# A gated mix of linear attention and a token-shifting MLP: the first x chunk turned by a DMA transpose, the opening loads reordered, later transposing loads cut smaller

## Chip, cores and metric

The kernel runs on one core of a Trainium2 chip. The metric is the device time of one execution in microseconds; the time before is the median of six runs.

## What is computed

The input x has 2048 rows of 640 columns (bfloat16). Branch A is linear attention with 32 heads of 20, branch B a token-shifting MLP; a sigmoid gate per row mixes them.

```python
x = A_x
g = sigmoid((x * gate_w).sum(-1, keepdims=True))

# branch A
q, k, v = heads of (x @ wqkv)                 # 640 -> 3 * 640
phi = lambda t: where(t > 0, t + 1, exp(t)) + 1e-6
pq, pk = phi(q), phi(k)
kv = einsum("bhsd,bhse->bhde", pk, v)
z = pk.sum(over rows)
a = (pq @ kv / (pq . z + 1e-6)) @ wo

# branch B
h = gelu(layernorm(x) @ w1)                   # then its four column groups are shifted
x1 = x + shifted(h) @ w2                      # by +1, -1, +2, -2 rows
b = x1 + gelu(layernorm(x1) @ w3) @ w4        # 640 -> 1728 -> 640

out = g * a + (1 - g) * b
```

## The kernel before

The 2048 rows are 16 chunks of 128 (`NCH`), the 640 columns five slices of 128 (`DC`). x is held twice: `x_sb` (tile RXH) with rows on the partitions, `xT` (tile RXT) turned, with columns on the partitions. The K weights lie in `wkg` (tile RA), 640 columns in five slabs by rows of wqkv. Two columns are added to them: column 640 is `gate_w`, so that the K product gives the gate's sum as well, and column 641 is one, which gives the row sums. `KW` is thus 642, and `k_mm(c, p, dc)` does one slice of chunk c in two matmuls, of 512 and of 130 columns, into the PSUM tile `PP[p]`. Each PSUM tile holds two banks of 512 columns.

All instructions of an engine run in the order in which the code issues them (`manual_schedule`); waits between engines are on semaphores. The stages follow one another on TensorE: K of all chunks (L334 to L350), with the first steps of G = x^T pk (`g_unit`, L261) mixed in from chunk 5 on; Q (L387) with the rest of G; w1 (L420), w2 (L553), and then w3 (L568), attention's product (L594) and w4 (L635) in two halves.

The opening works so:

- ACT's queue issues wk slabs 0, 1, 2 and 4, SP's queue x chunks 0, 1, 2 and wk slab 3 (L166 to L171). GpSimd's queue issues the load of `gate_w` into `g5` (L160).
- TensorE runs six warm-up matmuls on zeros (L305), then the transpose of a mask (L306), which ACT copies to `E4` (L307). It lies in `PP[0]`, the tile of chunk 0's K product.
- `x_tr(c, a, b)` turns chunk c on TensorE, five transposes into PSUM (L313), and copies the result to `xT`, three slices by VectorE (L314) and two by ACT (L315). Chunks 0, 1 and 2 go this way.
- After `x_tr(0, 3, 2)` a one-element memset on VectorE (L320) writes into chunk 3's place in `xT`. The transposing load of chunk 3 writes the same place, so SP waits there until the memset is done.
- `late_loads` then issues on SP, in one fixed order, the other chunks of x, transposing loads into `xT` (L157, from the input in device memory) taking turns with plain copies into `x_sb` (L154), and behind them wq (L290), w1, wv, wo and w2. `xT` of a chunk is read by that chunk's K product, `x_sb` by G and by the layernorm statistics.
- After `x_tr(1, 1, 2)` the gate's five values per partition are made by a transpose of `g5` (L324) and copied by VectorE into column 640 of the five slabs (L326). Then come K of chunk 0, slices 0 and 1, `x_tr(2, 3, 2)`, and the rest of K of chunks 0 to 2.

Of the kernel before, what the change touches and what calls it, by code (L numbers as in the profile page):

```python
# [16 lines left out]
def kernel(  # L17
# [27 lines left out]
    KW = D + 2  # L45
# [24 lines left out]
    x_sb = RXH[:, 0:NCH * D].rearrange("p (c d) -> p c d", c=NCH)  # L70
# [66 lines left out]
    def alloc():  # L137
        return free.pop(0)
# [11 lines left out]
    sp, aq = nc.sync, nc.scalar  # L150
    xv = x2.rearrange("(c p) d -> p c d", p=P)

    def load_x(c0, c1):
        sp.dma_start(x_sb[:, c0:c1, :], xv[:, c0:c1, :])  # L154

    def load_xT(c0, c1):
        sp.dma_start_transpose(xT[:, :, c0 * P:c1 * P], x2[c0 * P:c1 * P, :])  # L157
# [5 lines left out]
    def load_wk(q, dc):  # L163
        q.dma_start(wkg[:, dc, 0:D], A_wqkv[dc * P:(dc + 1) * P, D:2 * D])

    for dc in (0, 1, 2, 4):  # L166
        load_wk(aq, dc)
    load_x(0, 1)
    load_x(1, 2)
    load_x(2, 3)  # L170
    load_wk(sp, 3)  # L171


    nc.gpsimd.memset(mask4[:], 1.0)
# [72 lines left out]
        nc.vector.tensor_scalar(e[:, 0:n], e[:, 0:n], 1.0, 1e-6, op0=ALU.min, op1=ALU.add)  # L247
        nc.vector.scalar_tensor_tensor(dst, src, 0.0, e[:, 0:n], op0=ALU.max, op1=ALU.add)

    def k_mm(c, p, dc):  # L250
        for (n0, n1) in ((0, 512), (512, KW)):
            mm(PP[p][:, n0:n1], lhsT=xT[:, dc, c * P:(c + 1) * P], rhs=wkg[:, dc, n0:n1],  # L252
               start=(dc == 0), stop=(dc == DC - 1))

# [22 lines left out]
    def late_loads():  # L277
        load_xT(3, 4)
        load_xT(4, 5)
        load_x(3, 4)  # L280
        load_xT(5, 7)
        load_x(4, 6)
        load_xT(7, 9)
        load_x(6, 9)
        load_xT(9, 12)
        load_x(9, 12)
        load_xT(12, 16)
        load_x(12, 16)
        rows = lambda w, a, b: w[:, a:b].rearrange("(j p) d -> p j d", p=P)
        sp.dma_start(wq, rows(A_wqkv, 0, D))  # L290
        sp.dma_start(w1, rows(B_w1, 0, D))
        sp.dma_start(wv, rows(A_wqkv, 2 * D, 3 * D))
        sp.dma_start(wo6[0:GW, 0:5, :], A_wo[0:5 * GW, :].rearrange("(g r) d -> r g d", r=GW))
        sp.dma_start(wo6[0:gsz[5], 5, :], A_wo[5 * GW:D, :])
        sp.dma_start(w2[:, 0:4, :], B_w2.rearrange("(g c) d -> c g d", c=CG)[0:P])
        for g in range(4):
            sp.dma_start(w2[32 * g:32 * (g + 1), 4, :], B_w2[CG * g + P:CG * (g + 1), :])
        w1g = w1.rearrange("p k (g c) -> p k g c", c=CG)
        w1x4 = w1x.rearrange("p k (g c) -> p k g c", g=4)
        for g in range(4):  # L300
            nc.gpsimd.tensor_copy(w1x4[:, :, g, :], w1g[:, :, g, P:CG])


    for _ in range(6):
        mm(PP[3][:, 512:1024], lhsT=warm[:, 0:P], rhs=warm[:], start=True, stop=True)  # L305
    nc.tensor.transpose(PP[0][:, 0:64].bitcast(BF16), mask4[:], ident[:])  # L306
    act(E4[:], PP[0][:, 0:64].bitcast(BF16), ACT.Copy)  # L307
# [1 line left out]
    def x_tr(c, a, b):  # L309
        ta, tb = PP[a][:, 0:512].bitcast(BF16), PP[b][:, 0:512].bitcast(BF16)  # L310
        for dc in range(DC):
            t, k = (ta, dc) if dc < 3 else (tb, dc - 3)
            nc.tensor.transpose(t[:, k * P:(k + 1) * P], x_sb[:, c, dc * P:(dc + 1) * P], ident[:])  # L313
        nc.vector.tensor_copy(xT[:, 0:3, c * P:(c + 1) * P], ta[:, 0:3 * P].rearrange("p (j s) -> p j s", j=3))  # L314
        act(xT[:, 3:5, c * P:(c + 1) * P], tb[:, 0:2 * P].rearrange("p (j s) -> p j s", j=2), ACT.Copy)  # L315

    for _ in range(3):
        alloc()
    x_tr(0, 3, 2)
    nc.vector.memset(xT[:, 0, 3 * P:3 * P + 1], 0.0)  # L320
    late_loads()
    x_tr(1, 1, 2)
    tg = PP[3][:, 512:1024].bitcast(BF16)
    nc.tensor.transpose(tg[:, 0:DC], g5[0:DC, :], ident[0:DC, 0:DC])  # L324
    for dc in range(DC):
        nc.vector.tensor_copy(wkg[:, dc, D:D + 1], tg[:, dc:dc + 1])  # L326
    k_mm(0, 0, 0)
    k_mm(0, 0, 1)
    x_tr(2, 3, 2)
    k_mm(1, 1, 0)  # L330
    k_mm(1, 1, 1)
    k_mm(2, 2, 0)
    k_mm(2, 2, 1)
    for c in range(3):  # L334
# [7 lines left out]
    for c in range(3, NCH):  # L342
        p = alloc()
# [37 lines left out]
    for half in range(2):  # L381
        for j in range(DC):
            p = alloc()
# [301 lines left out]
```

## Time and profile before

| | us |
|---|---|
| time, median of 6 runs | 267.65 |
| lowest and highest of the 6 | 267.49, 268.2 |
| the profiled execution's own time | 268.05 |
| its span, from first to last instruction | 266.3 |
| TensorE busy (share of the span) | 261.0 (98%) |
| VectorE, ACT, GpSimd busy | 116.0, 110.7, 32.8 |
| granted TensorE clock, mean | 1.0 |

The span is what the profile's views cover; the time is that of the whole execution as the device reports it. Times in the views are counted from the first instruction. TensorE's busy time counts matmuls from start to modelled end, so overlapping ones are counted once. A line such as L252 is the line of the code that issued the instruction; where a helper is called from many places, they share its line. An instruction of a DMA queue (SPq, ACTq) is shown for the time that it held the issuing queue, and its landing is given apart, counted from the start of the issue.

### The profile page before, as it was taken

How to read it: one execution, taken by the hardware profiler on the slowest of the kernel's cores; microseconds unless marked ns; L12 is line 12 of the kernel's file. 1: busy time of each engine (PE TensorE's matmuls, PEld its weight loads, DVE VectorE, ACT ScalarE, POOL GpSimd, SP SyncE). 2: the span in 40 equal slices, each digit the busy share in tenths (PEclk: the TensorE clock that was granted, in tenths of full speed). 3: DMA queues.
4: the chain of work that ended last, by engine and by line, in shares of the span. 5: the costliest groups of instructions: out<-in, count | busy, mean ns of one | idle time of the engine just before them, and what ended most of it. 6: DMA issues, size and time to landing. Idle time of an engine off the chain costs nothing.

```text
span 266.3 us, 4224 instructions
## 1 busy us (share of the span) xinstructions
PE 261.0 (98%) x1699; PEld 135.4 (51%) x1699; DVE 116.0 (44%) x212; ACT 110.7 (42%) x165; POOL 32.8 (12%) x111
## 2 busy tenths in 40 slices
PE   6999999999999999999999999999999999999995
PEld 2555555555545445554444455555544444555552
DVE  2486748665655065999920033233200002233232
ACT  3466663665355771244977522022034444022020
POOL 5000222020200000536870000000000000000000
PEclk9999999999999999999999999999999999999999
DMA  6999993431340269942652001001000000001001
GB/s 203 182 233 252 362 225 67 62 75 25 77 98 0 60 214 363 312 81 49 101 100 49 0 2 49 27 25 49 27 25 0 2 0 0 25 27 49 27 25 49
DMA packets 42149, 23.95 MB, mean 90 GB/s; under 512 B 30994, under 2 KB 41362, under 8 KB 42130
## 3 DMA queue, kind: packets, MB, share of 16 engines
q1 hardware_dynamic: 41378, 22.99, 35.2%
q10 hardware_dynamic: 720, 0.69, 0.8%
q8 instruction: 13, 0.21, 0.4%
q14 instruction: 6, 0.05, 0.1%
q0 software_dynamic: 32, 0.00, 0.0%
HBM read 12.86 MB, written 3.44 MB: 61 GB/s over the span
## 4 chain that ended last, share of the span: by engine, by line
PE 96%; DMA 2%; DVE 0%; issue 0%; POOLq 0%
PE pp L635 20%; PE pp L568 19%; PE pp L252 8%; PE pp L420 8%; PE pp L594 8%; PE pp L387 8%; PE pp L553 8%; PE pp L261 8%; DMA g<-in_gate_w_dram 2%; PE pp L577 2%; PE pp L620 1%; PE pp L629 1%; PE pp L584 1%; PE pp L454 1%; PE pp L440 1%; PE pp L361 0%
## 5 line engine op out<-in xcount | busy, mean ns | idle before, releaser
L635 PE MATMUL pp<-RB,RXH 128*128 128x512 bf16 (+1 forms) x390 | 54.4, 299 | 0.0
L568 PE MATMUL pp<-lnxT,RA 128*128 128x512 bf16 x240 | 52.1, 379 | 0.0
L635 PEld LDWEIGHTS <-RXH 128*128 128x128 bf16 x390 | 29.6, 98 | 24.2 <-issue 2.1
L568 PEld LDWEIGHTS <-RA 128*128 128x128 bf16 x240 | 23.4, 98 | 28.0
L597 ACT ACTIVATE RXH<-pp,g_all 128x640 f32<-128x640 f32 x16 | 12.7, 793 | 54.9 <-PE pp L594 54.9
L570 ACT ACTIVATE RXH<-pp 128x1024 bf16<-128x1024 f32 x24 | 24.2, 1019 | 26.7 <-PE pp L568 26.7
L244 ACT ACTIVATE eb<-pp 128x640 bf16<-128x640 f32 (+1 forms) x26 | 21.4, 828 | 25.3 <-PE pp L387 16.3
L261 PE MATMUL pp<-RPK,RXH 128*128 128x512 bf16 (+1 forms) x160 | 25.2, 299 | 0.0
L252 PE MATMUL pp<-RA,RXT 128*128 128x512 bf16 (+1 forms) x160 | 24.0, 300 | 0.0
L387 PE MATMUL pp<-RXT,RA 128*128 128x512 bf16 x100 | 23.3, 379 | 0.0
L594 PE MATMUL pp<-Mp,pqT 128*128 128x512 bf16 (+1 forms) x160 | 23.1, 299 | 0.0
L599 DVE SCALAR_TENSOR_TENSOR RPK<-RPK,omg,RXH 128x640 f32<-128x640 f32 x8 | 7.1, 885 | 36.5 <-ACT RXH L597 36.5
L553 PE MATMUL pp<-w,RXH 128*128 128x512 bf16 (+1 forms) x160 | 21.9, 299 | 0.0
L420 PE MATMUL pp<-lnxT,RB 128*128 128x512 bf16 x80 | 18.3, 379 | 0.0
L261 PEld LDWEIGHTS <-RXH 128*128 128x128 bf16 x160 | 12.7, 98 | 10.4
L247 DVE TENSOR_SCALAR eb<-eb 128x640 bf16<-128x640 bf16 (+1 forms) x26 | 9.5, 364 | 19.4 <-ACT eb L244 19.4
L599 DVE SCALAR_TENSOR_TENSOR RXT<-RXT,omg,RXH 128x640 f32<-128x640 f32 x8 | 7.1, 885 | 24.6 <-ACT RXH L597 24.6
L594 PEld LDWEIGHTS <-pqT 128*128 128x128 bf16 x160 | 12.2, 98 | 10.0 <-issue 0.8
L252 PEld LDWEIGHTS <-RXT 128*128 128x128 bf16 x160 | 12.3, 98 | 9.6 <-DVE RA L326 0.2
L553 PEld LDWEIGHTS <-RXH 128*128 128x128 bf16 x160 | 12.3, 98 | 9.5
L604 DVE SCALAR_TENSOR_TENSOR RXH<-pp,omg,RXT 128x640 bf16<-128x640 f32 x8 | 7.1, 884 | 19.8 <-PE pp L635 19.8
L387 PEld LDWEIGHTS <-RA 128*128 128x128 bf16 x100 | 11.1, 118 | 8.9
(110 smaller groups left out, 237.4 us busy)
## 6 DMA issues: line engine op xcount, KB each, us to landing
out_dram<-RXH SPq DMA_DIRECT2D x15, 160.0 KB, 1.8
RA<-in_B_w_dram SPq DMA_DIRECT2D x5, 432.0 KB, 7.0
RA<-in_A_wqkv_dram SPq DMA_DIRECT2D x2, 800.0 KB, 8.6
RB<-in_B_w_dram SPq DMA_DIRECT2D x1, 1120.0 KB
RXH<-in_A_x_dram SPq DMA_DIRECT2D x2, 480.0 KB, 4.9
RB<-in_B_w_dram SPq DMA_DIRECT2D x1, 960.0 KB, 12.8
RB<-in_B_w_dram SPq DMA_DIRECT2D x1, 800.0 KB, 8.2
Mp<-Mscr SPq DMA_DIRECT2D x1, 800.0 KB
```

Source lines behind the costliest of these rows:

```text
L244: act(e[:, 0:n], src, ACT.Exp)
L252: mm(PP[p][:, n0:n1], lhsT=xT[:, dc, c * P:(c + 1) * P], rhs=wkg[:, dc, n0:n1], start=(dc == 0), stop=(dc == DC - 1))
L261: mm(PP[p][:, n0:n1], lhsT=x_sb[:, c, i * P:(i + 1) * P], rhs=pk[:, c, n0:n1], start=(c == 0), stop=(c == NCH - 1))
L387: mm(PP[p][:, tt * 512:(tt + 1) * 512], lhsT=wqp[:, dc, j], rhs=xT[:, dc, t0:t0 + 512], start=(dc == 0), stop=(dc == DC - 1))
L420: mm(PP[p][:, tt * 512:(tt + 1) * 512], lhsT=lh, rhs=lnxT[:, dc, t0:t0 + 512], start=(dc == 0), stop=(dc == DC - 1))
L553: mm(PP[p][:, n0:n1], lhsT=hsT[:, fc, 2 + c * P:2 + (c + 1) * P], rhs=w2[:, fc, n0:n1], start=(fc == 0), stop=(fc == DC - 1))
L568: mm(PP[p][:, k * 512:(k + 1) * 512], lhsT=w3[:, dc, (fc + k) * P:(fc + k + 1) * P], rhs=lnxT[:, dc, t * 512:(t + 1) * 512], start=(dc == ...
L570: act(h2T[:, t % 2, fc:fc + 2, :], PP[p][:].rearrange("p (k s) -> p k s", k=2), ACT.Gelu_apprx_tanh)
L594: mm(PP[p][:, n0:n1], lhsT=pqT[:, j, c * P:(c + 1) * P], rhs=Mp[:, j, n0:n1], start=(j == 0), stop=(j == DC - 1))
L597: act(ga, PP[p][:, 0:D], ACT.Copy, scale=g_all[:, c:c + 1])
L599: nc.vector.scalar_tensor_tensor(x1(c), x1(c), omg[:, c:c + 1], ga, op0=ALU.mult, op1=ALU.add)
L635: mm(PP[p][:, n0:n1], lhsT=h2T[:, k, fc, cc], rhs=w4[:, fc, n0:n1], start=False, stop=(fc == NF - 1))
```

## The change

Chunk 0 is no longer loaded as rows and turned on TensorE: a transposing load of chunk 0 into `xT` is the first instruction on SP's queue. x chunks 1 and 2 move to ACT's queue, between wk slabs 0 and 1 and after slab 1; slabs 2, 3 and 4 are on SP's, behind the transpose. A seventh warm-up matmul is added. `k_mm` gets an argument that chooses the 512-wide or the 130-wide part: for chunks 0 and 1, slices 0 and 1, the wide parts are issued first, two of them ahead of the gate's transpose, and the four narrow parts, which read the gate column, afterwards. `x_tr(0, ...)` is gone, the marker memset stands after `x_tr(1, 1, 2)`. In `late_loads` a plain copy of chunk 0 into `x_sb` is added, and the transposing loads are of 1, 1, 1, 1, 1, 2, 1, 2 and 3 chunks, where they were of 1, 1, 2, 2, 3 and 4. What is computed is the same.

```diff
-    for dc in (0, 1, 2, 4):
-        load_wk(aq, dc)
-    load_x(0, 1)
-    load_x(1, 2)
-    load_x(2, 3)
-    load_wk(sp, 3)
+    load_xT(0, 1)
+    load_wk(aq, 0)
+    aq.dma_start(x_sb[:, 1, :], xv[:, 1, :])
+    load_wk(aq, 1)
+    aq.dma_start(x_sb[:, 2, :], xv[:, 2, :])
+    for dc in (2, 3, 4):
+        load_wk(sp, dc)
...
-    def k_mm(c, p, dc):
-        for (n0, n1) in ((0, 512), (512, KW)):
+    def k_mm(c, p, dc, part=(0, 1)):
+        for (n0, n1) in (((0, 512), (512, KW))[k] for k in part):
...
         load_xT(3, 4)
         load_xT(4, 5)
+        load_x(0, 1)
         load_x(3, 4)
-        load_xT(5, 7)
+        load_xT(5, 6)
+        load_xT(6, 7)
         load_x(4, 6)
-        load_xT(7, 9)
+        load_xT(7, 8)
+        load_xT(8, 10)
         load_x(6, 9)
-        load_xT(9, 12)
+        load_xT(10, 11)
+        load_xT(11, 13)
         load_x(9, 12)
-        load_xT(12, 16)
+        load_xT(13, 16)
         load_x(12, 16)
...
-    for _ in range(6):
+    for _ in range(7):
         mm(PP[3][:, 512:1024], lhsT=warm[:, 0:P], rhs=warm[:], start=True, stop=True)
...
-    x_tr(0, 3, 2)
+    k_mm(0, 0, 0, (0,))
+    x_tr(1, 1, 2)
     nc.vector.memset(xT[:, 0, 3 * P:3 * P + 1], 0.0)
     late_loads()
-    x_tr(1, 1, 2)
+    k_mm(0, 0, 1, (0,))
     tg = PP[3][:, 512:1024].bitcast(BF16)
     nc.tensor.transpose(tg[:, 0:DC], g5[0:DC, :], ident[0:DC, 0:DC])
     for dc in range(DC):
         nc.vector.tensor_copy(wkg[:, dc, D:D + 1], tg[:, dc:dc + 1])
-    k_mm(0, 0, 0)
-    k_mm(0, 0, 1)
+    k_mm(1, 1, 0, (0,))
     x_tr(2, 3, 2)
-    k_mm(1, 1, 0)
-    k_mm(1, 1, 1)
+    k_mm(1, 1, 1, (0,))
+    for c in range(2):
+        for dc in range(2):
+            k_mm(c, c, dc, (1,))
     k_mm(2, 2, 0)
     k_mm(2, 2, 1)
```

## The prediction

> **What bounds the kernel now.** I began with the page's slices: TensorE is full from the second slice to the end.
>
> ```profile
> PE   6999999999999999999999999999999999999995
> ```
>
> Only the first of the 40 slices (6.66 us each) has idle time. So the change can gain only before TensorE becomes dense, and it loses whatever idle time it opens later. The timeline of TensorE shows where that is (columns: start us, us, engine, line, operation, tiles, shape, count, idle time and releaser).
>
> ```profile
> 4.11 0.45 PE L313 MATMUL pp<-ident,RXH 128*128 128x128 bf16 x5
> 4.82 0.49 PE L313 MATMUL pp<-ident,RXH 128*128 128x128 bf16 x5 [0.26 <-DMA RXH<-in_A_x_dram]
> 5.95 0.17 PE L324 MATMUL pp<-ident,g 5*128 5x5 bf16 x1 [0.64 <-DMA g<-in_gate_w_dram]
> 6.06 0.83 PE L252 MATMUL pp<-RA,RXT 128*128 128x512 bf16 x4
> 6.72 0.45 PE L313 MATMUL pp<-ident,RXH 128*128 128x128 bf16 x5
> 7.00 7.88 PE L252 MATMUL pp<-RA,RXT 128*128 128x512 bf16 x56
> 14.72 0.71 PE L261 MATMUL pp<-RPK,RXH 128*128 128x512 bf16 x4
> ...
> 18.95 1.52 PE L252 MATMUL pp<-RA,RXT 128*128 128x512 bf16 x10
> ...
> 27.17 1.52 PE L252 MATMUL pp<-RA,RXT 128*128 128x512 bf16 x10
> ...
> 32.07 2.32 PE L387 MATMUL pp<-RXT,RA 128*128 128x512 bf16 x10
> ```
>
> To be seen: the first K matmul (L252) waits until 6.06, although chunks 0 and 1 were turned by 5.3, because the gate column's transpose (L324) stands ahead of it and its DMA landed at 5.9. From 7.00 nothing is idle. The chain of waits has 1.36 us for the ten K matmuls of a chunk, 0.272 for a pair of 512 and 130 columns. So chunk 5 starts 1.36 before 14.72, at 13.36, and chunk 3 at 10.64: **the first three chunks end at 10.64**, and the sum is made against that. Then the SP queue, which issues every transposing load:
>
> ```profile
> 0.80 1.34 SPq L154 DMA_DIRECT2D RXH<-in_A_x_dram  x3
> ...
> 4.90 2.61 SPq L157 DMA_TRANSPOSE RXT<-in_A_x_dram  x2
> 7.56 0.58 SPq L154 DMA_DIRECT2D RXH<-in_A_x_dram  x1
> 8.18 1.52 SPq L157 DMA_TRANSPOSE RXT<-in_A_x_dram  x1
> ...
> 12.37 4.46 SPq L157 DMA_TRANSPOSE RXT<-in_A_x_dram  x1
> ...
> 22.63 0.51 SPq L290 DMA_DIRECT2D RA<-in_A_wqkv_dram  x1
> ```
>
> To be seen: a transpose of one chunk holds SP for 1.30 us, of two chunks 1.34 to 1.52, of three or four 4.46, a copy 0.58. SP is never idle from 4.90 to 22.63, so every added issue moves all later loads. Last, landings, asked one transposing load at a time (chunk 3, then chunks 7 and 8):
>
> ```profile
> L157 SPq DMA_TRANSPOSE RXT<-in_A_x_dram x1: 1297/1297/1297, 4.9 to 4.9; - x1
> ...
> DMA to landing us min/median/max: 3.6/3.6/3.6
> ```
>
> ```profile
> L157 SPq DMA_TRANSPOSE RXT<-in_A_x_dram x1: 1337/1337/1337, 10.4 to 10.4; - x1
> ...
> DMA to landing us min/median/max: 5.1/5.1/5.1
> ```
>
> The others, asked likewise: chunk 4 3.1, chunks 5 and 6 3.8, chunks 12 to 15 6.5, wq 6.5; plain x0 3.3, x1 3.5, x2 4.9; on ACT wk0 3.5, wk1 3.8, wk2 5.2.
>
> **The change, part by part.** *Chunk 0 by DMA transpose.* It goes out at 0.80, x0's old place. The trace has no transpose in the opening rush. Bounds: 3.1 (chunk 4's, few copies about), so 3.9, and 6.5 (the largest), so 7.3. I take 5.1, landing at **5.9**: that transpose shared its queue with a copy of two chunks, and this one has four copies on ACT's queue beside it all the way; 3.6 had only the tail of copies, and that the 5.1 carried two chunks speaks for less. Below 4.8 an early landing is worth nothing: the seventh warm-up matmul (about 0.4) moves the mask's transpose from 3.79 to some 4.1, and K's first matmul writes the bank that the E4 copy reads, which ended 0.63 after that transpose began.
>
> The Trainium skill speaks for the change here: "Advanced Engine Details and Errata", section X-Bar Transpose (TRN2), says that transposing DMAs run as fast as regular ones. By it chunk 0 would land like x0, 3.3 after its issue, and the sum would be the first rival's; the rows of 3.6 and 5.1 beside 2.9 for the copy of chunk 3 disagree, and I go by them.
>
> *TensorE's new order.* Five transposes fall away (0.28, by 6.72 to 7.00), but they lay in time lost to the gate anyway: worth nothing by themselves. The two 512-wide K products now put ahead of the gate cost 2 x 0.216 (ten of L387 take 2.16) and fill that idle time. Step by step from 5.9: K(0,0) to 6.12; x1's transposes to 6.40; K(0,1) to 6.62 (wk1, third on ACT, lands between 1.72 + 3.8 = 5.5 and 1.72 + 5.2 = 6.9; I take 6.2, between them, since the transpose ahead on the other queue replaces a copy); the gate to 6.73. K(1,0) needs x1's copy out of PSUM, ended 0.74 after the transposes' start each time (4.11 to 4.85), so 6.12 + 0.74 = 6.86, with the hand-over 6.9, and runs to 7.12. x2's transposes to 7.40 (x2, fourth on ACT, landed 6.7 from SP before; by 7.1 it would still be in time), K(1,1) to 7.62. Four 130-wide products in a row go at the pace of their weight loads, 0.098 each (the page's L252 loads) in place of 0.056: to 8.01. Eleven of fifteen pairs remain: 2.99. **End of three chunks: 11.00, that is 0.36 later.** The gate's five DVE columns (0.42) lie under x2's transposes; if not covered they would cost that much.
>
> *The late loads.* The marker memset (L320) now comes after x1's transposes, not x0's, and SP waits for it: x1's transposes start at 6.12, and 0.79 later (4.11 to 4.90) chunk 3 is issued: 6.91, **2.01 later**. Behind it on SP is every load up to w2. Chunk 3 lands at 10.5 for 11.0, chunk 4 at 11.4 for 12.4. Chunk 5 follows 1.35 + 1.32 + 2 x 0.63 (x0's copy is new here) = 3.93 after, at 10.84. It lands between 13.9 (3.1) and 14.6 (3.8, for two chunks behind a copy); I take 3.2, one chunk, at 14.04. It is needed at 11.00 + 2.72 = 13.72: **stall 0.32**. All later needs then stand 0.68 later. Smaller pieces from there: 1.30 + 1.30 + 0.57 + 1.30 + 1.45 + 0.57 + 1.30 + 1.45 + 0.57 + 4.46 + 0.58 and 11 gaps of 0.05 = 15.4, so wq goes out at 26.2 (22.63 before) and lands at 32.7; its first reader stands at 32.07 + 0.68 = 32.75. Chunks 13 to 15 go out at 21.1, land by 27.6 for 27.85. So the slack is used up but nothing is added: 0 here, up to 1.0 in the last rival.
>
> *Slabs shared over both queues.* wk2 to wk4 stand behind the transpose on SP, and are first read after 8.5; the last slabs' old issue at 2.2 plus 5.2 gives 7.4. They cost nothing unless they land over a microsecond later.
> The Trainium skill, "DMA: Bandwidth & Descriptors", section Issuing engines are not separate DMA queues, says that a second issuing engine saves only issue time. Second loads of 3.5 on SP and 3.8 on ACT fit that; by it this part brings 0, as in the sum.
>
> **Sum.** 0.36 + 0.32 = 0.68 later. The profiled execution took 268.05 (span 266.3 and 1.75 around it), so its like would take 268.7; it stands 0.4 over the median of the six runs, 267.65, so the median is forecast at **268.3**. What can be told from no change is about 0.2%, 0.54 us.
>
> **Rivals.** *1. The transpose lands early* (3.6 or less: 4.4). Then TensorE starts at 4.8, x1's transposes end at 5.3, wk1 is there at 5.5 and the gate still arrives at 5.9: K(1,0) from 6.06 to 6.28, x2 to 6.6, K(1,1) and the narrow ones to 7.2, the end 10.2: 0.45 gained. If the gate too comes at 5.3, with fewer rows ahead of it, and x2 by 5.9, 0.35 more. SP's marker is then 5.8, chunk 5 lands at 12.9 for 12.6 to 12.9, which takes back up to 0.3. Middle 0.6: 267.05. For it: chunk 3's 3.6. Against: four copies beside.
>
> *2. It cancels.* Landing near 5.2: the end is 10.3, chunk 5 at 13.3 for 13.0: 0.0 to 0.3 gained or lost, 267.6. The gate's wait hides the new start. This is also the case in which the change does not bring the earlier start it says.
>
> *3. A late piece on the crowded SP queue* stops TensorE. Place: chunks 8 and 9, issued at 15.5. With 3.8 they land at 19.3 for 18.95 + 0.68 = 19.6; with 5.1, as behind a copy before, at 20.6. It decides from a landing of 4.1 upward; price 1.0 on top: 269.3, slower. For it: the same place in the order (just behind a copy and a transpose). Against: the copy's data may be through by then.
>
> **Chances.** Forecast 0.41, rival 1 0.25, rival 2 0.22, rival 3 0.12. Slower by over 0.2%: forecast and rival 3, 0.53; within: 0.22; faster: 0.25. The forecast's own range is 268.1 to 268.8 (landing at 5.7 to 6.3). To leave out no more than two in ten, the range must reach to half of rival 1 and of rival 3: 266.95 to 269.4.
>
> **What would show it.** In the new profile: chunk 0's transpose landing 5.1 after 0.80, the first L252 matmul near 5.9 (a start at 4.8 to 5.0 is rival 1); L157's first late issue near 6.9; TensorE waiting on RXT at some 13.7; wq issued near 26; no wait after 33. If chunk 0 lands before 4.9, or TensorE's first three chunks end before 10.3, the prediction is wrong in its first term; if SP catches up by 22.6, in its second.

## The result: slower, by more than forecast

The changed kernel takes 269.77 us (median of 21 runs, 268.65 to 271.5), before 268.00 (median of 43, 267.48 to 268.96). The ratio is 1.0063, 95% interval [1.0052, 1.0073]: **1.7 us slower**, where 0.68 was forecast, and the median lies over the upper end of the range, 269.4. The profiled execution of after took 270.44, 0.7 over the median of its kernel; its span is 268.7, 2.4 over that of before.

The page's slices look as before: TensorE full from the second slice on, and the granted clock (PEclk) at full in every slice.

```profile
span 268.7 us, 4218 instructions
...
PE   6999999999999999999999999999999999999995
...
PEclk9999999999999999999999999999999999999999
```

The loss is in the first slice and just behind it. TensorE's timeline of after (columns as in the prediction; L253 is now the K product, L318 the turning of a chunk, L330 the gate's transpose, L262 the first G step):

```profile
4.21 0.31 PE L311 MATMUL pp<-ident,mask 128*128 128x128 bf16 x1
5.46 0.61 PE L253 MATMUL pp<-RA,RXT 128*128 128x512 bf16 x1 [0.94 <-DMA RXT<-in_A_x_dram]
5.87 0.74 PE L318 MATMUL pp<-ident,RXH 128*128 128x128 bf16 x5
7.21 0.59 PE L253 MATMUL pp<-RA,RXT 128*128 128x512 bf16 x1 [0.61 <-DMA RA<-in_A_wqkv_dram]
7.73 0.18 PE L330 MATMUL pp<-ident,g 5*128 5x5 bf16 x1
7.85 0.61 PE L253 MATMUL pp<-RA,RXT 128*128 128x512 bf16 x1
8.43 0.69 PE L318 MATMUL pp<-ident,RXH 128*128 128x128 bf16 x5
8.92 8.54 PE L253 MATMUL pp<-RA,RXT 128*128 128x512 bf16 x57
17.30 0.71 PE L262 MATMUL pp<-RPK,RXH 128*128 128x512 bf16 x4
```

Three things are to be seen. The first K product starts at 5.46, 0.6 earlier than before's 6.06, so the early transpose does what it was put there for. Then TensorE stands still for slab 1 of the K weights until 7.21, and everything behind it in order waits too: the gate, chunk 1, chunk 2. And a matmul of 512 columns is shown at 0.61 or 0.59 us; before, matmuls of this kind were at most 0.39. The first G step comes at 17.30 in place of 14.72, 2.58 later; after that the gaps between the stages are those of before. No wait of TensorE follows 9 us.

The loads that were late, each by itself (slab 1, third on ACT, and chunk 2, fourth):

```profile
L164 ACTq DMA_DIRECT2D RA<-in_A_wqkv_dram x1: 460/460/460, 1.7 to 1.7; - x1
DMA to landing us min/median/max: 5.5/5.5/5.5
...
L170 ACTq DMA_DIRECT2D RXH<-in_A_x_dram x1: 654/654/654, 2.2 to 2.2; - x1
...
DMA to landing us min/median/max: 5.9/5.9/5.9
```

Before, slab 1 was second on ACT and took 3.8, chunk 2 third on SP and took 4.9. The transpose of chunk 0 landed 4.6 after its issue, at 5.4.

The SP queue of after went almost as forecast:

```profile
0.79 1.30 SPq L157 DMA_TRANSPOSE RXT<-in_A_x_dram  x1
2.15 1.51 SPq L164 DMA_DIRECT2D RA<-in_A_wqkv_dram  x3
6.84 2.54 SPq L157 DMA_TRANSPOSE RXT<-in_A_x_dram  x2
...
26.38 0.51 SPq L295 DMA_DIRECT2D RA<-in_A_wqkv_dram  x1
```

Chunk 3 is issued at 6.84 (6.91 forecast) and wq at 26.38 (26.2). But TensorE was later still, so nothing waited for these loads.

The rate of TensorE is seen best from the weight loads of the K product, first those that start between 5.4 and 10.4 us of after, then those from 10.8 on (min, median and max in ns):

```profile
L253 PEld LDWEIGHTS <-RXT x12: 102/147/152, 5.5 to 10.3; 128*128 128x128 bf16 x12
```

```profile
L253 PEld LDWEIGHTS <-RXT x18: 97/98/98, 10.8 to 13.2; 128*128 128x128 bf16 x18
```

Up to about 10.5 us a weight load takes 0.147 and a wide matmul holds TensorE for 0.41 (from 5.46 to 5.87), later 0.098 and 0.216: **about half rate** by the wide matmuls. The trace's clock records say the same: their first entry, full rate, stands at 10.65 in after and at 4.15 in before. The row PEclk does not show it, since the time ahead of the first record counts as full there.

### The profile page after: what moved, and what is told of

The parts are those of the page before. It is cut to its first block, busy times and chain, and to the rows that moved or that the text cites. A ratio compares the mean times of both kernels' runs of the same rounds, so it can differ in the third digit from the quotient of the medians.

```text
span 268.7 us, 4218 instructions
## 1 busy us (share of the span) xinstructions
PE 262.9 (98%) x1695; PEld 136.2 (51%) x1695; DVE 115.6 (43%) x211; ACT 110.3 (41%) x164; POOL 32.7 (12%) x111
## 4 chain that ended last, share of the span: by engine, by line
PE 96%; DMA 2%; DVE 0%; ACTq 0%; issue 0%
PE pp L642 20%; PE pp L575 19%; PE pp L253 9%; PE pp L427 8%; PE pp L601 8%; PE pp L394 8%; PE pp L262 8%; PE pp L560 8%; DMA RA<-in_A_wqkv_dram 2%; PE pp L584 2%; PE pp L627 1%; PE pp L636 1%; PE pp L591 1%; PE pp L461 1%; PE pp L447 1%; PE pp L368 0%
## 5 line engine op out<-in xcount | busy, mean ns | idle before, releaser
L253 PE MATMUL pp<-RA,RXT 128*128 128x512 bf16 (+1 forms) x160 | 25.6, 311 | 1.5 <-DMA RXT<-in_A_x_dram 0.9
L262 PE MATMUL pp<-RPK,RXH 128*128 128x512 bf16 (+1 forms) x160 | 25.2, 299 | 0.0
L253 PEld LDWEIGHTS <-RXT 128*128 128x128 bf16 x160 | 12.9, 101 | 11.1 <-DMA RXT<-in_A_x_dram 1.5
L262 PEld LDWEIGHTS <-RXH 128*128 128x128 bf16 x160 | 12.7, 98 | 10.4
```

What stands on the lines that cost most here:

```text
L262: mm(PP[p][:, n0:n1], lhsT=x_sb[:, c, i * P:(i + 1) * P], rhs=pk[:, c, n0:n1], start=(c == 0), stop=(c == NCH - 1))
```

## Experiments

The theory formed from this: the loss is all in the opening, one part from loads that land later because of their new places in the queues, one part from a TensorE clock that stays at half rate because of the holes, the idle stretches between its instructions. The rivals: the late pieces on SP (the prediction's second step), the new order on TensorE, the transpose itself beside the copies. Ratios are those to before, measured side by side with it.

| run | ratio | 95% interval |
|---|---|---|
| after | 1.0063 | [1.0052, 1.0073] |
| e1_pieces | 0.9996 | [0.9985, 1.0008] |
| e2_opening | 1.0085 | [1.0068, 1.0102] |
| e3_plain0 | 1.0051 | [1.0036, 1.0066] |
| e4_extra_transpose | 1.0170 | [1.0153, 1.0187] |
| e5_queues_back | 1.0019 | [1.0010, 1.0028] |
| e6_after_filled | 1.0035 | [1.0023, 1.0047] |
| e7_wide_first | 0.9988 | [0.9979, 0.9997] |
| e8_wide_filled | 0.9999 | [0.9990, 1.0008] |
| e9_wk1_second | 1.0069 | [1.0049, 1.0089] |
| e10_transpose_in_place | 1.0088 | [1.0059, 1.0117] |
| e11_no_warm_up | 1.0038 | [1.0014, 1.0062] |

**e1_pieces**, before with the smaller pieces alone:

```diff
-        load_xT(5, 7)
+        load_xT(5, 6)
+        load_xT(6, 7)
         load_x(4, 6)
-        load_xT(7, 9)
+        load_xT(7, 8)
+        load_xT(8, 10)
...
```

> The opening of before with the late transposing loads cut as in after (1, 1, 2, 1, 2, 3 chunks from chunk 5 on). Theory, the opening alone costs (late slabs and a slow TensorE clock): the same as before within 0.3 us, no wait of TensorE on xT after 9 us. The prediction's second step (the late loads on SP stall TensorE): some slack lost but no stall with SP's start at 4.9; also the same. So this run only bounds the price of the pieces: 0 expected by both, over 0.5 us slower would speak for a third cause.

0.9996: the pieces cost nothing in before's place. **e2_opening** is the counterpart, after with the late pieces of before (the same lines the other way round):

> The opening of after with the late pieces of before (from chunk 5 on 2, 2, 3, 4 chunks). Theory, the opening alone costs: the whole loss stays, 1.5 to 2.0 us slower than before. Prediction's second step: 0.3 us of the loss comes back, 1.3 to 1.5 us slower.

1.0085: the whole loss stays, nothing comes back. Its interval reaches a little into that of after, so that it is worse than after is not shown. The late pieces have no part in the loss of after. The profile of this run shows more than that:

```profile
6.23 0.58 PE L253 MATMUL pp<-RA,RXT 128*128 128x512 bf16 x1 [0.17 <-DMA RA<-in_A_wqkv_dram]
...
16.64 0.71 PE L262 MATMUL pp<-RPK,RXH 128*128 128x512 bf16 x4
```

Slab 1 landed at 6.19 here and chunk 2 at 7.14, as early as the prediction had them, and yet the first G step comes 1.92 after before's. Full rate stands from 10.33 only, with no more than 0.56 us of idle time in the opening.

**e3_plain0**, after with chunk 0 loaded as a plain copy and turned on TensorE (its late copy falls away):

```diff
-    load_xT(0, 1)
+    load_x(0, 1)
     load_wk(aq, 0)
...
+    x_tr(0, 3, 2)
     k_mm(0, 0, 0, (0,))
     x_tr(1, 1, 2)
```

> After with chunk 0 loaded as a plain copy first on SP and turned on TensorE ahead of the first K product; everything else as in after, slabs and x 1, 2 in after's queues (the plain copy of chunk 0 in the late loads falls away). Theory, the transpose beside the copies delays wk1 and x2: wk1 lands by 5.6 to 6.2 instead of 7.2 and the time is within 0.5 us of before. Rival, the sharing of slabs over the queues and the third place of wk1 on ACT delay it: wk1 still lands near 7 and the time stays over 1 us slower than before.

The rival's outcome: 1.0051, with slab 1 still landing at 6.8 and chunk 2 at 7.6. TensorE's timeline of this run:

```profile
5.70 0.61 PE L317 MATMUL pp<-ident,RXH 128*128 128x128 bf16 x5
6.83 0.38 PE L253 MATMUL pp<-RA,RXT 128*128 128x512 bf16 x1 [0.53 <-DMA RA<-in_A_wqkv_dram]
```

The same wait for slab 1, with no transpose in the opening at all. My theory had put the delay down to the transpose beside the copies; that fell. The intervals of this run and of after overlap, so a price of the transpose beyond the new places (the difference is 0.3 us) is not shown by this pair.

**e4_extra_transpose**, before with a transpose of chunk 15 ahead of all else on SP:

```diff
+    load_xT(15, 16)
     for dc in (0, 1, 2, 4):
         load_wk(aq, dc)
...
-        load_xT(12, 16)
+        load_xT(12, 15)
```

> Before with one transposing load more in the opening: chunk 15, needed only at the end of the K stage, goes out first on SP, and the last late load is one chunk shorter. TensorE's order is that of before. Theory, a transpose beside the opening's copies slows them: x0 to x2 and wk1 land 0.5 to 1.5 us later than in before, and the time is 0.7 to 2 us slower. Rival, only the new order on TensorE costs: the copies land as in before but for SP's 1.3 us issue, 0.4 to 1.0 us slower at most.

1.0170, 4.6 us: far beyond both expectations. The timeline:

```profile
6.58 1.56 PE L314 MATMUL pp<-ident,RXH 128*128 128x128 bf16 x10 [2.48 <-DMA RXH<-in_A_x_dram]
```

Chunk 0, now second on SP, landed at 6.5 and not at 4.1, and after the hole of 2.48 full rate came at 11.8 us by the clock records. A transpose ahead of a needed copy on one queue thus costs that copy some 2.4 us, of which 1.3 are its issue.

**e5_queues_back**, e3_plain0 with the queues of before:

```diff
-    load_x(0, 1)
-    load_wk(aq, 0)
-    aq.dma_start(x_sb[:, 1, :], xv[:, 1, :])
-    load_wk(aq, 1)
-    aq.dma_start(x_sb[:, 2, :], xv[:, 2, :])
-    for dc in (2, 3, 4):
-        load_wk(sp, dc)
+    for dc in (0, 1, 2, 4):
+        load_wk(aq, dc)
+    load_x(0, 1)
+    load_x(1, 2)
+    load_x(2, 3)
+    load_wk(sp, 3)
```

> As e3_plain0 (chunk 0 plain, TensorE's order of after), but the opening's loads in before's queues: x 0, 1, 2 and slab 3 on SP, slabs 0, 1, 2, 4 on ACT. Theory, the places in the queues cost (wk1 third on ACT and chunk 2 fourth, against second and third): wk1 lands near 5.0 and chunk 2 near 6.7, and the time is within 0.4 us of before. Rival, TensorE's new order costs: still 1.0 to 1.4 us slower.

1.0019, a little over the 0.4 us of the theory, and 0.9 us faster than e3_plain0, whose interval lies wholly above: **the places in the queues are worth 0.9 us**. The clock has no part in it in the two profiles: from the second K product (slab 1) to the first G step both take 9.0, but it starts at 5.59 here and at 6.83 in e3_plain0. For what is left over before, the timeline of e5_queues_back has a likely cause:

```profile
14.59 0.71 PE L261 MATMUL pp<-RPK,RXH 128*128 128x512 bf16 x4
...
17.70 1.54 PE L252 MATMUL pp<-RA,RXT 128*128 128x512 bf16 x10 [0.36 <-DMA RXT<-in_A_x_dram]
```

The first G step is 0.13 earlier than in before's profile, so this opening shows no loss; but chunk 7 now waits 0.36 for its transposed load. SP's late loads started at 6.1 here. The mechanism of the prediction's second step exists; it can show when TensorE's opening is quick enough.

**e6_after_filled**, after with four matmuls on zeros in its holes:

```diff
     act(E4[:], PP[0][:, 0:64].bitcast(BF16), ACT.Copy)
+    for _ in range(2):
+        mm(PP[3][:, 512:1024], lhsT=warm[:, 0:P], rhs=warm[:], start=True, stop=True)
...
     late_loads()
+    for _ in range(2):
+        mm(PP[3][:, 512:1024], lhsT=warm[:, 0:P], rhs=warm[:], start=True, stop=True)
     k_mm(0, 0, 1, (0,))
```

> After with four matmuls on zeros more: two behind the mask's transpose, two ahead of K of chunk 0, slice 1, where TensorE waits for loads. The loads are not touched. Theory, half of the loss is the clock (full rate from 10.7 us instead of 4.2, since the holes keep it down): full rate from about 5 to 8 us and 0.6 to 1.2 us faster than after, 0.5 to 1.1 slower than before. Rival, only the late loads cost: no faster than after, or slower by up to 0.4.

1.0035: useless work added, and 0.75 us faster than after (0.0028 of 268; the intervals do not touch). In its profile full rate stands from 4.3 us. The opening's loads do not depend on TensorE, so a clock that is full sooner is the one way that idle work can help: **somewhat less than half of the loss is thus the clock's**. This rests on the medians. The one profile would not do for it, since its loads landed at the early end of what the others show (slab 1 at 6.3, chunk 2 at 7.1), and landings differ from execution to execution.

**e7_wide_first**, before with another order on TensorE and nothing else (`k_mm` gets after's argument for its parts):

```diff
...
     x_tr(1, 1, 2)
+    k_mm(0, 0, 0, (0,))
+    k_mm(0, 0, 1, (0,))
     tg = PP[3][:, 512:1024].bitcast(BF16)
...
-    k_mm(0, 0, 0)
-    k_mm(0, 0, 1)
-    x_tr(2, 3, 2)
-    k_mm(1, 1, 0)
-    k_mm(1, 1, 1)
-    k_mm(2, 2, 0)
-    k_mm(2, 2, 1)
-    for c in range(3):
-        k_mm(c, c, 2)
+    k_mm(1, 1, 0, (0,))
+    k_mm(1, 1, 1, (0,))
+    for c in range(2):
+        for dc in range(2):
+            k_mm(c, c, dc, (1,))
+    x_tr(2, 3, 2)
+    k_mm(0, 0, 2)
+    k_mm(1, 1, 2)
+    for dc in range(3):
+        k_mm(2, 2, dc)
```

> Before with nothing but the order on TensorE changed: loads and queues as in before; the wide products of chunk 0, slices 0 and 1, ahead of the gate's transpose, those of chunk 1 and the four narrow ones behind it, then the turning of chunk 2, then slice 2 of chunks 0 and 1, then chunk 2. Worked out from before: idle time before the gate takes 0.43, the narrow ones cost 0.17 more, no wait for chunk 2's copy: 0.2 to 0.5 us faster than before. Rival, the gate and chunk 2 set the pace in any order: the same within 0.15.

0.9988 [0.9979, 0.9997]: 0.3 us, as expected, and the only version here whose interval lies below both kernels, if barely: it allows gains from 0.08 to 0.56 us, so the rival's "within 0.15" is not excluded, and its profile has the first G step at 14.73, where before's has it at 14.72. The useful idea of the change, K products that need no gate ahead of the gate, costs nothing when no load is moved for it, and perhaps gains a little.

**e8_wide_filled** adds two matmuls on zeros to e7_wide_first:

```diff
-    for _ in range(6):
+    for _ in range(7):
...
     k_mm(0, 0, 1, (0,))
+    mm(PP[3][:, 512:1024], lhsT=warm[:, 0:P], rhs=warm[:], start=True, stop=True)
```

> e7_wide_first with a seventh warm-up matmul and one more on zeros ahead of the gate's transpose, so that TensorE has no hole before 6 us. Theory of the clock: the full rate comes earlier in more of the executions, so a smaller spread and 0 to 0.4 us faster than e7_wide_first. Rival, before's holes are too short to matter: the same, or slower by the 0.2 that a filler takes.

0.9999: no gain is shown; nearer the rival. The intervals of the two runs overlap, so that the fillers cost something is not shown either.

**e9_wk1_second**, after with slab 1 and chunk 1 exchanged on ACT:

```diff
-    aq.dma_start(x_sb[:, 1, :], xv[:, 1, :])
     load_wk(aq, 1)
+    aq.dma_start(x_sb[:, 1, :], xv[:, 1, :])
...
     k_mm(0, 0, 0, (0,))
+    k_mm(0, 0, 1, (0,))
     x_tr(1, 1, 2)
...
-    k_mm(0, 0, 1, (0,))
```

> After with slab 1 second and chunk 1 third on ACT's queue, and the wide product of slice 1 right behind that of slice 0, ahead of chunk 1's turning. Theory, what stands third on a queue lands near 6 to 7 whatever it is: slab 1 lands near 5.0, chunk 1 between 6.0 and 7.2, TensorE now waits for chunk 1, and the time stays 1.3 to 2.2 us slower than before. Rival, slab 1 itself is the cost: 0.5 to 1.0 of the loss comes back.

1.0069: as slow as after. In the landings the theory holds: slab 1, now second, landed at 4.87, and chunk 1, now third, at 5.95, where it had landed at 4.97 as second in after. So it is the third place that is late, not slab 1. In the time the run is less clear. TensorE waited 0.1 for chunk 1 in this profile, and the first G step, at 15.29, is 0.58 earlier than in the quicker profile of after (e12_after_again below). That gain was taken back by a late piece, at chunk 8:

```profile
20.29 1.54 PE L253 MATMUL pp<-RA,RXT 128*128 128x512 bf16 x10 [0.76 <-DMA RXT<-in_A_x_dram]
```

**e10_transpose_in_place**, after with before's queues, the transpose standing where chunk 0's copy stood:

```diff
-    load_xT(0, 1)
-    load_wk(aq, 0)
...
+    for dc in (0, 1, 2, 4):
+        load_wk(aq, dc)
+    load_xT(0, 1)
+    load_x(1, 2)
+    load_x(2, 3)
+    load_wk(sp, 3)
```

> After with before's queues, the transpose of chunk 0 standing in the place of its plain copy: SP has the transpose, chunks 1 and 2 and slab 3, ACT slabs 0, 1, 2 and 4. Beside e5_queues_back this changes the transpose alone. Theory, the transpose holds SP for 1.3 us and delays what follows on its queue: chunk 1 lands at 6.0 to 6.8 instead of 4.5, and the time is 1.5 to 2.5 us slower than before. Rival, the transpose costs little and the sharing was the loss: within 0.8 us of before.

1.0088, 2.4 us: as the theory had it. Beside e5_queues_back only the transpose differs, and what comes with it: no turning of chunk 0 on TensorE, and its plain copy among the late loads on SP. The difference is 0.0069, or 1.8 us, by intervals that do not touch. So the transpose has a price in this place: it lands later than before's copy (5.1 against 4.1) and holds back chunk 1 behind it (6.4 against 4.5), for which TensorE waited 0.92. Part of the 1.8 are late pieces, for which this profile waited 0.84 and that of e5_queues_back 0.36. After's sharing takes chunk 1 out of its way, and pays with slab 1.

**e11_no_warm_up**, before without its six warm-up matmuls:

```diff
-    for _ in range(6):
-        mm(PP[3][:, 512:1024], lhsT=warm[:, 0:P], rhs=warm[:], start=True, stop=True)
```

> Before without its six warm-up matmuls; loads and order as in before, only the granted clock differs. Theory of the clock: full rate comes at 7 to 11 us instead of 4 to 7, and the time is 0.8 to 1.5 us slower than before. Rival, the clock does not matter here: the same within 0.3 us.

1.0038, 1.0 us: no load and no needed instruction differs from before, which leaves the clock as the cause. Its profile, with full rate from 7.5, was one of its quick executions (268.13, first G step at 14.89) and does not show the loss itself.

**e12_after_again**, after unchanged, one more profile:

> After once more, unchanged, for a second profile of it: theory, in it too chunk 0 lands by 5.5, slab 1 at 6.0 to 7.2 and chunk 2 at 7.0 to 8.1, no wait of TensorE after 9 us, and the span follows the moment from which the clock is full.

It took 269.02, with a span of 267.3. Slab 1 landed at 6.84 and chunk 2 at 7.70, as late as expected, but full rate stood from 4.96:

```profile
5.21 0.39 PE L253 MATMUL pp<-RA,RXT 128*128 128x512 bf16 x1 [0.69 <-DMA RXT<-in_A_x_dram]
5.44 0.44 PE L318 MATMUL pp<-ident,RXH 128*128 128x128 bf16 x5
6.88 0.38 PE L253 MATMUL pp<-RA,RXT 128*128 128x512 bf16 x1 [1.00 <-DMA RA<-in_A_wqkv_dram]
...
7.88 0.44 PE L318 MATMUL pp<-ident,RXH 128*128 128x128 bf16 x5 [0.19 <-DVE RA L332]
8.15 7.88 PE L253 MATMUL pp<-RA,RXT 128*128 128x512 bf16 x56
15.87 0.71 PE L262 MATMUL pp<-RPK,RXH 128*128 128x512 bf16 x4
```

The wait for slab 1 is there (1.00), the matmuls have before's 0.39, and the first G step comes at 15.87. Against the first profile of the same program that is 1.43 earlier, and the span is 1.4 shorter. Of the 1.43, 0.33 lie ahead of the second K product (6.88 against 7.21, by the landing of slab 1), and 1.10 behind it, where only the rate differs. The loss that remains at full rate is 1.15 (15.87 against 14.72).

Chunk 2 was late in both profiles, but it is not what TensorE waited for last: its turning starts at 7.88, behind the copies of the gate's columns (L332), which ended at 7.82; the chunk had landed at 7.70. In the first profile these are 8.43, 8.37 and 8.03.

## Why the prediction was wrong

The side was right, the size was not. The sum's step from the second K product, K(0,1), to the first G step can be set beside the four profiles that have after's opening loads. The sum has K(0,1) at 6.40, the end of three chunks at 11.00 and, three chunks of 1.36 later, the first G step at 15.08, without its late piece:

| | slab 1 landed | K(0,1) starts | from there to the first G step | full rate from |
|---|---|---|---|---|
| the sum | 6.2 | 6.40 | 8.68 | taken as given |
| after | 7.17 | 7.21 | 10.09 | 10.65 |
| e12_after_again | 6.84 | 6.88 | 8.99 | 4.96 |
| e2_opening | 6.19 | 6.23 | 10.41 | 10.33 |
| e6_after_filled | 6.29 | 6.33 | 8.99 | 4.28 |

**One failing step is the landing of slab 1, the third load on ACT.** The prediction took 6.2, "between them, since the transpose ahead on the other queue replaces a copy", and priced the sharing of the loads over both queues at 0. Slab 1 landed at 7.2 and 6.8 in after's two profiles, 0.48 to 0.81 late for K(0,1), and at 6.2 and 6.3 in the two others: it varies, and the sum took a value from its early end. The upper bound of its own range, from the row of a third load (5.2), was 6.9, and the nearest row was that one; the step to the middle had no row behind it. That the places cost is shown by e3_plain0 against e5_queues_back, 0.9. Chunk 2, let pass with "by 7.1 it would still be in time", landed at 8.0 and 7.7, but cost nothing of its own.

**The other is a term that was missing: the clock.** Every product was priced at full rate, as in before. Where full rate came early, the way from K(0,1) to the first G step takes 8.99, 0.31 over the sum; where it came after 10 us, 1.1 to 1.4 more. In e2_opening, with slab 1 on time, this is nearly the whole error. That the median pays for the clock is shown by e6_after_filled, 0.75 faster with idle work added, and by e11_no_warm_up. Before's rows had the warning in them: the first warm-up matmuls start 0.43 apart, and the row of weight loads on zeros has a mean of 138 ns, against 98 later. The sum never asked what TensorE's new idle time would do to that.

The holes are not the whole reason for a late clock: e2_opening had 0.56 us of idle time between 3.9 and 8 us and full rate from 10.33, e12_after_again 1.88 us and full rate from 4.96. By the clock records of all fourteen profiles, full rate lasts either 262.83 or 259.41 us, whatever the span (265.8 to 270.0). The two lengths differ by 3.42 us, and this suggests that the rate changes only in steps of some 3.4 us, whose place differs from execution to execution.

The Trainium skill has the rule: "TensorE: Matmul & The Clock Gate", section Part 1: The HAM clock gate, says that the rate starts at half and is released by one busy window of some 3.4 us, that the windows run freely of the program's start, and that an idle window sends it back. The runs agree on half rate by duration (0.41 against 0.216), on the length by the 3.42 above, and on the free start, with one and the same program at full rate from 4.96 in one execution and from 10.65 in another. How busy a window must be is not shown by these runs.

**A small term was read as covered and was not.** The 0.31 that is left at full rate is for the most part the gate's five columns, which were to "lie under x2's transposes": the turning of chunk 2 waits for them, 0.19 in e12_after_again, e6_after_filled and e3_plain0 alike. The rest is 0.09 between K(0,1) and the gate, and 0.03 in all that follows: order, the price of the narrow matmuls and that of the eleven pairs held.

**The first term's premise was too dark and did not decide.** The transpose landed at 5.42 and 5.17, where 5.9 was taken; that is rival 2's landing. (It took 4.1 to 4.6 in all profiles that have it there, a plain copy in its place 2.7 to 3.3.) Rival 2 gave 0.0 to 0.3 for it. It was refuted by slab 1, which stood between chunk 0 and everything else: the forecast and rivals 1 and 2 hung on the landing of chunk 0, and that was not the last thing that TensorE waited for.

**The second term, 0.32 from late pieces, was zero in after**, as e1_pieces and e2_opening show, though SP's times were right to 0.3. The step compared them with a TensorE that was to be at 11.0 and was at 13.2 and 11.8. The mechanism is real: 0.36 in e5_queues_back, 0.76 in e9_wk1_second, and 0.25 and 0.59 in e10_transpose_in_place, at chunk 7, at chunk 8, and at chunks 5 and 8. So rival 3's mechanism stood ready, two of the four waits in the place that it named. An opening that is quick while SP's late loads start late can meet it; e6_after_filled, with its first G step at 15.32 and SP's start at 6.10, did not.

**Where the 1.7 us come from**, then: about 0.75 by the clock (after against e6_after_filled), and about 0.95 that stay when idle work is added (e6_after_filled against before). That these are the loads that landed later is argued, not shown: the new order and the fillers lie in them too. The places in the queues are worth 0.9 by themselves with chunk 0 as a copy (e3_plain0 against e5_queues_back). The last pair shares no kernel with the others, so its 0.9 stands beside the 0.95 and is not a part measured within it.

## What to carry to other kernels

For an opening that is bound by loads, list what each engine needs in order and count the place of each load in its queue. Where no transpose stood ahead, second places landed by 5.1 here and third ones at 5.9 to 7.2 whatever they held; second places behind a transpose landed at 6.4 to 7.4. One move that helps the first need pushes another behind it. Price idle time on TensorE in the first ten microseconds at more than its length, since it can also put off full rate, and expect the moment to differ between executions; a profile's durations show this where its clock row does not. To fill a wait with work that needs nothing new (e7_wide_first) is the cheaper thing to try before any load is moved, though its own gain here is hardly measurable.

## What the hardware showed that was not expected

- The moment of full rate varies: it lay between 4.15 and 11.8 us in the fourteen profiles of this case, and the two profiles of after show what that can do to the time. After's 21 runs spread over 2.9 us, before's 43 over 1.5, but 22 further ones of before, beside e9_wk1_second, over 2.7 (one of them at 269.88, the rest within 1.2).
- A load can be late by its last part alone. Each of these loads reports sixteen times in the trace's semaphore records; fifteen of slab 1 in after had come by 5.64 and the last came at 7.17; of chunk 2, 6.69 and 8.03. In before it was 5.93 and 6.67 for chunk 2. In e2_opening and e6_after_filled the last one of slab 1 was only 0.07 and 0.04 behind. So 1.5 of slab 1's 5.5 us in after are one straggling part; why it straggles was not tried, and how far it belongs to the place in the queue stays open.
- A transpose first on SP (e4_extra_transpose) made the copy behind it land 2.4 us later, 4.4 after its own issue instead of 3.3, although the transposed chunk is no larger than the copy.
